# Spacer tiles between the moving operands of the four large products of an attention and two-layer feed-forward kernel

## The chip, the cores and the metric

One core of one Trainium2 chip runs the whole program. The metric is the device time in microseconds; lower is better. TensorE (PE) does the matrix products, VectorE (DVE), ScalarE (ACT) and GpSimd (POOL) the elementwise work, and SyncE (SP) issues the DMAs.

## The reference

```python
scores = scale * np.matmul(q, k.transpose(0, 1, 3, 2))       # 4 batches, 8 heads, 576 tokens, 64 wide
scores = np.where(block_i >= block_j, scores, -1000000000.0)  # blocks of 64 tokens
attn = np.exp(scores - np.max(scores, axis=-1, keepdims=True))
attn = attn / (np.sum(attn, axis=-1, keepdims=True) + 1e-09)
x = np.matmul(attn, v).transpose(0, 2, 1, 3).reshape(2304, 512)
...
g = x @ w_gate                                                # 512 x 1536
x = (g / (1 + np.exp(-g)) * (x @ w_val)) @ w_out              # 1536 x 512
...
h = x @ w_in                                                  # 512 x 2048
out = np.where(h > 0, h, np.exp(np.minimum(h, 0)) - 1) @ w_out2   # 2048 x 512
```

All tensors are float32.

## The kernel before

The 2304 tokens are worked on in three phases. Every large product is made three times as precise as one pass by splitting both operands into a high and a low part (float32r): `mm3` (lines 163 to 166) issues high weights times high operand (L164), high weights times low operand (L165) and low weights times high operand (L166). For TensorE one operand is stationary (the "weights", 128 columns, loaded by an LDWEIGHTS ahead of the matmul) and one is moving (streamed through, up to 512 columns). While a matmul streams its moving operand, the next matmul's weights are loaded.

- Phase 1, to about 482 us: attention, and the product **gv** (gate and value, `gv_pair`). It goes over 9 chunks of 256 tokens; the moving operand is `xh` or `xl` (a tile of 4 x 256 columns, three buffers of each, chunk c uses buffer c mod 3), the weights are `wh` and `wl`.
- Phase 2, to about 655 us: the product **y** (`p2_unit`): five chunks, four of 512 and one of 256 tokens. The moving operand is `ah` or `al` (three buffers each), the weights `woh` and `wol`. Meanwhile `p3_weights` prepares weights for phase 3.
- Phase 3, to the end: the products **h** and **o**, over 3 groups of 768 tokens and 8 pairs of 128 hidden columns. h (`p3_h`) is written as seven products of halves (a Strassen-like scheme): the moving operand is `yo0` to `yo6` (384 columns of a high or low part), the weights are streamed slots `ws`, six matmuls for each of the seven. o (`p3_o`, L891 to L893) has the second layer's weights `oh`/`ol` as the moving operand (512 columns) and the activations `gh`/`gl` (the last three of eight buffers are `ah`/`al` again) as the stationary one. o trails h by one step, and runs of the two alternate.

The order of all instructions on all engines is fixed by `Plan.order`, a planner with costs written in the kernel; it knows nothing of addresses. Addresses come from pools that are filled tile after tile from either end of the memory. A tile that takes the place of an older one waits for the older one's readers. In this kernel all weights of the four products start at 128 bytes modulo 512. `padr` (352 bytes), `padx` (192) and `padw` (320) are tiles that nobody reads: they shift what is allocated behind them.

Of the kernel before, what the change touches and what calls it, by code (L numbers as in the profile page):

```python
# [8 lines left out]
F32 = mybir.dt.float32  # L9
F32R = mybir.dt.float32r  # L10
# [11 lines left out]
KD, K1, K2 = DM // 128, F1 // 128, F2 // 128  # L22
BLK = 64
CH = 256
# [13 lines left out]
HT, NG, HP, PAIR3, NP, NW, NE = 384, 3, K2 // 2, 15.4, 8, 8, 3  # L38
# [72 lines left out]
def attention_moe_moe_kernel(ctx: ExitStack, tc: tile.TileContext,  # L111
# [9 lines left out]
    def sb(name, bufs, side="left"):  # L121
        return tc.alloc_tile_pool(name=name, bufs=bufs, side=side, reuse_waits="tile")

    def ps(name, bufs, side="left"):
        return tc.alloc_tile_pool(name=name, bufs=bufs, side=side, space=PSUM, reuse_waits="tile")

    const = sb("const", 1)
    ident = const.tile([128, 128], F32, name="ident")
    conv = sb("conv", 1)
# [82 lines left out]
    pl_t = {g: [attn.tile([128, e], F32, name=f"pl{g}{i}") for i in range(2)] for g, e in ((0, 256), (1, 512))}  # L212
    ph_t = [attn.tile([128, S], F32, name=f"ph{i}") for i in range(2)]
    x_p = sb("x", 1)
    x_p.tile([128, 48], F32, name="padx")
    ph1 = sb("ph1", 1)
    ph1.tile([128, 80], F32, name="padw")
    t0 = sb("t0", 1)
    lo_r, hi_r = slice(0, 64), slice(64, 128)
    xh_c, xl_c = {}, {}  # L220

    def x_alloc(c):
        if c not in xh_c:
            xh_c[c] = x_p.tile([128, KD, CH], F32R, tag="xh", name="xh", bufs=3)
            xl_c[c] = x_p.tile([128, KD, CH], F32R, tag="xl", name="xl", bufs=3)


    def conv_unit(i, prio, after=(), whole=False):
# [54 lines left out]
    def t0_attn(s, q):  # L283
# [50 lines left out]
        def x(p):  # L334
            x_alloc(0)
            cs = slice(128 * s, 128 * s + 128)
            xh, xl = (t[0][:, 2 * q:2 * q + 2, cs].rearrange("p j (u t) -> p u j t", u=2) for t in (xh_c, xl_c))
            src = st["pv"][:, :, 0:128].rearrange("p u (j t) -> p u j t", j=2)
            if p == 0:
                act.copy(xh, src)  # L340
            else:
                dve.tensor_tensor(xl, src, xh.bitcast(F32), ALU.subtract)
# [48 lines left out]
    def a_head(n, prio):  # L391
# [199 lines left out]
        def xh():  # L591
            x_alloc(ch)
            act.copy(xh_c[ch][:, k], xfs[i])
# [4 lines left out]
        if fp:  # L598
            def fh():
                x_alloc(ch)  # L600
                act.copy(xh_c[ch][xr, k], st["pv"][0:64, 0:QW])

            def fl():
                dve.tensor_tensor(xl_c[ch][xr, k], st["pv"][0:64, 0:QW], xh_c[ch][xr, k].bitcast(F32), ALU.subtract)  # L604

            add("ACT", 264, fh, prio, [pvk], [("x", ch, ("h", k))])
            add("DVE", 335, fl, prio, [pvk, ("x", ch, ("h", k))], [("x", ch, ("l", k))])
            return
# [46 lines left out]
    ar_b, ah_b, al_b, ys_b = [], [], [], []  # L655
# [74 lines left out]
    def w2_alloc(p, f):  # L730
        OH[f] = p.tile([128, DM], F32R, name=f"oh{f}")
        OL[f] = p.tile([128, DM], F32R, name=f"ol{f}")
        cv_units[unit["o", f]] = (w2o[f], OH[f], OL[f])
# [190 lines left out]

    def p2_bufs(p, r, h):
        ar_b.extend(p.tile([128, 512], F32, name=f"ar{k}") for k in r)
        ah_b.extend(p.tile([128, 512], F32R, name=f"ah{k}") for k in h)
        al_b.extend(p.tile([128, 512], F32R, name=f"al{k}") for k in h)

    def to_w1():  # L930
        attn.release()
        at_ps.release()
        hand["st2"] = sb("st2", 1, "right")
        p2_bufs(hand["st2"], (0, 1, 2), (0, 1, 2))
        hand["w1"] = sb("w1", 1, "right")
        hand["y_ps"] = ps("y_ps", 1, "right")
        for g in range(K1 - 1):
            wo_alloc(hand["w1"], g)

    def wo_alloc(p, g):  # L940
        WOH[g] = p.tile([128, DM], F32R, name=f"woh{g}")
        WOL[g] = p.tile([128, DM], F32R, name=f"wol{g}")
        cv_units[2 * K1 + g] = (wo[g], WOH[g], WOL[g])

    def to_p2():
        hand["wgvB"].release()
        ph1.release()
        x_p.release()
        wgvA.release()
        gv_ps.release()  # L950
        hand["st3"] = sb("st3", 1)
        p = hand["st3"]
        p2_bufs(p, (3, 4), ())
        wo_alloc(p, K1 - 1)
        ys_b.extend(p.tile([128, 512], F32, name=f"ys{k}") for k in range(4))
        p = hand["wp"] = sb("wp", 1)
        for f in range(2 * NE):
            w2_alloc(p, f)
        for r in range(4):
            yqt[r] = p.tile([128, 2, HT], F32, name=f"yq{r}")  # L960
        for o in range(6):
            yot[o] = p.tile([128, 2, 2, HT], F32R, name=f"yo{o}")
        hand["h_ps"] = ps("h_ps", 1)
        for k in range(2):
            hb[k] = hand["h_ps"].tile([128, 512], F32, name=f"h{k}")

    def to_p3():
        hand["w1"].release()
        hand["y_ps"].release()
        p = hand["wq"] = sb("wq", 1, "right")  # L970
        yot[6] = p.tile([128, 2, 2, HT], F32R, name="yo6")
        for f in range(2 * NE, K2):
            w2_alloc(p, f)
        for k in range(NP):
            gp[k] = [t[k - NP + 3][:, 0:HT] for t in (ah_b, al_b)] if k >= NP - 3 else [p.tile([128, HT], F32R, name=f"g{h}{k}") for h in "hl"]
        hand["o_ps"] = ps("o_ps", 1, "right")
        for j in range(6):
            ob[j] = hb[j + 2] = hand["o_ps"].tile([128, DM], F32, name=f"o{j}")
# [5 lines left out]
    for c, f in order:  # L984
        u = UNIT0 if c < 2 else UNIT
# [38 lines left out]
    for u, (c, f) in enumerate(order):  # L1024
# [4 lines left out]
        plan.group = None  # L1029
    add("NONE", 0, to_w1, PT0, writes=[("w1", 0, 0)], behind="attn")  # L1030
    add("NONE", 0, to_p2, PT0, writes=[("p2", 0, 0)], behind="gv")
    for g in range(K1):
        conv_unit(2 * K1 + g, due2[0, g] - CLEAD2, after=[("w1" if g < K1 - 1 else "p2", 0, 0)])
# [5 lines left out]
    for i, T in chunks:  # L1039
        for f in range(K1):  # L1040
            p2_unit(i, T, f, p2_prep(i, T, f), due2[i, f])
        p2_drain(i, T)
    add("NONE", 0, to_p3, PT0, writes=[("p3", 0, 0)], behind="p2")
    for p in range(NE, HP):
        for f in (2 * p + 1, 2 * p):
# [66 lines left out]
```

## Time and profile before

| | us |
|---|---|
| median of 3 runs | 1047.3 |
| lowest, highest | 1046.73, 1049.97 |
| span of the profiled execution, first to last instruction | 1045.0 |
| PE busy, share of the span | 98% |
| weight loads busy | 89% |
| DVE busy | 79% |

The span is the profiled execution's own time on the core; 2.3 us lie between it and the median. Recorded matmuls overlap (they are pipelined, and the ends are modelled), so that a matmul's duration is longer than the time from its start to the next one's start. The mean of a group is in nanoseconds.

### The profile page before, as it was taken

The numbers are of one execution on the slowest core, as the hardware profiler recorded it, in microseconds if no ns is written. First come the engines' busy times: TensorE is split into PE (matmuls) and PEld (weight loads), VectorE is DVE, ScalarE is ACT, GpSimd is POOL, SyncE is SP. The second block draws the span as 40 slices with busy tenths as digits, with TensorE's granted clock in tenths as the row PEclk, the third lists the DMA queues.
The fourth block names the chain that finished last, engine by engine and source line by source line (L and its number), as shares of the span: only waits on it lengthen the run. The fifth ranks groups of instructions, "written<-read, shape, count | busy, mean of one in ns | idle before, by whom it ended". The sixth has DMA issues, their size and how long they took to land.

```text
span 1045.0 us, 19569 instructions
## 1 busy us (share of the span) xinstructions
PE 1023.0 (98%) x6520; PEld 935.1 (89%) x6520; DVE 825.7 (79%) x1967; ACT 606.3 (58%) x1531; POOL 286.5 (27%) x288
## 2 busy tenths in 40 slices
PE   9999899999999999999999999999999999999998
PEld 8678899999999999999977888898888998898897
DVE  6889999988888888877666775889998666876665
ACT  3898787776776677654354555555563443543343
POOL 1267543443444344303233222223210000000000
PEclk9999999999999999999999999999999999999999
DMA  7577557422542254004779988777646433454331
GB/s 177 163 217 207 154 160 202 122 80 87 139 123 81 85 140 122 25 28 134 227 258 321 316 292 282 252 237 235 218 149 211 126 121 121 122 172 121 112 111 61
DMA packets 119366, 170.00 MB, mean 163 GB/s; under 512 B 15840, under 2 KB 75744, under 8 KB 119264
## 3 DMA queue, kind: packets, MB, share of 16 engines
q1 hardware_dynamic: 119264, 168.74, 53.3%
q8 instruction: 52, 0.85, 0.3%
q14 instruction: 50, 0.41, 0.1%
HBM read 130.42 MB, written 38.27 MB: 161 GB/s over the span
## 4 chain that ended last, share of the span: by engine, by line
PE 79%; DVE 11%; DMA 4%; ACT 2%; issue 2%; SPq 1%; POOL 0%; ACTq 0%; DVEq 0%; POOLq 0%
PE gv L164 8%; PE gv L166 7%; PE gv L165 7%; PE o L893 6%; PE o L892 6%; PE o L891 6%; PE h L165 5%; PE h L166 5%; PE h L164 5%; PE y L165 3%; PE y L164 3%; PE y L166 3%; PE tr L534 2%; PE tr L533 2%; PE pv L551 2%
## 5 line engine op out<-in xcount | busy, mean ns | idle before, releaser
L164 PE MATMUL gv<-xh,wh 128*128 128x256 f32 x864 | 255.8, 296 | 0.2
L165 PE MATMUL gv<-xl,wh 128*128 128x256 f32 x864 | 241.7, 280 | 0.1
L166 PE MATMUL gv<-xh,wl 128*128 128x256 f32 x864 | 241.4, 279 | 0.0
L164 PEld LDWEIGHTS gv<-xh,wh 128*128 128x128 f32 x864 | 163.6, 189 | 4.8 <-issue 3.4
L165 PEld LDWEIGHTS gv<-xl,wh 128*128 128x128 f32 x864 | 163.8, 190 | 0.5 <-DVE xl L604 0.3
L166 PEld LDWEIGHTS gv<-xh,wl 128*128 128x128 f32 x864 | 163.3, 189 | 0.2 <-POOL wl L161 0.2
L853 DVE TENSOR_TENSOR ys<-h,ys 128x384 f32<-128x384 f32 x162 | 88.1, 554 | 69.1 <-PE h L166 66.3
L844 ACT ACTIVATE ar<-ys 128x384 f32<-128x384 f32 x96 | 50.4, 525 | 113.0 <-DVE ys L853 94.9
L165 PE MATMUL h<-yo,ws 128*128 128x384 f32 x326 | 110.1, 338 | 0.6 <-DVE yo L757 0.6
L164 PE MATMUL h<-yo,ws 128*128 128x384 f32 x326 | 109.3, 335 | 0.6 <-ACT ys L864 0.6
L166 PE MATMUL h<-yo,ws 128*128 128x384 f32 x326 | 109.6, 336 | 0.0
L409 POOL TENSOR_TENSOR ks<-rk,ks 64x576 fp32r<-64x576 f32 (+1 forms) x56 | 70.6, 1261 | 90.6 <-ACT ks L406 49.5
L165 PE MATMUL y<-al,woh 128*128 128x512 f32 (+1 forms) x240 | 89.0, 371 | 1.3 <-DVE al L669 1.1
L164 PE MATMUL y<-ah,woh 128*128 128x512 f32 (+1 forms) x240 | 88.5, 369 | 0.2 <-ACT ys L708 0.2
L166 PE MATMUL y<-ah,wol 128*128 128x512 f32 (+1 forms) x240 | 88.4, 368 | 0.0
L803 POOL TENSOR_TENSOR wm<-c,wm 128x256 fp32r<-128x256 f32 x56 | 50.6, 910 | 130.9 <-ACT wm L800 122.9
L538 ACT CAST th<-tr 128x256 fp32r<-128x256 f32 x176 | 61.3, 375 | 24.2 <-PE tr L534 22.8
L542 DVE TENSOR_TENSOR tl<-tr,th 128x256 fp32r<-128x256 f32 x176 | 69.0, 415 | 7.2 <-ACT th L538 6.5
L422 POOL TENSOR_TENSOR vs<-rv,vs 128x320 fp32r<-128x320 f32 (+1 forms) x56 | 47.2, 844 | 96.6 <-ACT vs L418 81.6
L892 PE MATMUL o<-ol,gh 128*128 128x512 f32 x180 | 71.2, 395 | 1.4 <-POOL ol L161 1.4
L893 PE MATMUL o<-oh,gl 128*128 128x512 f32 x180 | 71.5, 397 | 0.8 <-DVE gl L850 0.8
L891 PE MATMUL o<-oh,gh 128*128 128x512 f32 x180 | 70.2, 390 | 0.2 <-ACT oh L157 0.2
(149 smaller groups left out, 2673.5 us busy)
## 6 DMA issues: line engine op xcount, KB each, us to landing
ws<-w_scr SPq DMA_DIRECT2D x168, 256.0 KB, 2.7
w_scr<-wm SPq DMA_DIRECT2D x56, 256.0 KB, 3.9
a_scr<-as SPq DMA_DIRECT2D x54, 256.0 KB, 2.3
ar<-a_scr SPq DMA_DIRECT2D x108, 128.0 KB, 3.7
rk<-in_kt_dram SPq DMA_DIRECT2D x32, 288.0 KB, 4.4
raw<-in_w2i_dram SPq DMA_DIRECT2D x16, 512.0 KB, 4.7
raw<-in_w2o_dram SPq DMA_DIRECT2D x16, 512.0 KB, 4.3
rq<-in_qt_dram SPq DMA_DIRECT2D x60, 128.0 KB, 3.9
```

The costliest lines, as they stand in the source:

```text
L164: pe.matmul(dst, wh, xh, start=start, stop=False)
L165: pe.matmul(dst, wh, xl, start=False, stop=False)
L166: pe.matmul(dst, wl, xh, start=False, stop=stop)
L409: pool.tensor_tensor(st["ks"][64:128, 0:ext], raws[i][0][64:128, j, 0:ext], st["ks"][64:128, 0:ext].bitcast(F32), ALU.subtract)
L538: act.copy(st["th", c], st["tr", c][:, 0:QW])
L542: dve.tensor_tensor(st["tl", c], st["tr", c][:, 0:QW], st["th", c].bitcast(F32), ALU.subtract)
L803: add("POOL", 1000, lambda: pool.tensor_tensor(wm[n][:, 1], part(*x), wm[n][:, 0].bitcast(F32), ALU.subtract), prio, [ck(*x), hk] + whole, ...
L844: add("ACT", 500, lambda: act.activation(t(), src(), ACTF.Tanh, scale=0.5), PMP, [sk], [tk], first)
L853: add("DVE", 560, lambda: dve.tensor_tensor(hc(d), hb[b][:, 0:HT], hc(x), ALU.add), PMP, [hbk(b), hck(x)], [hck(d)])
L891: pe.matmul(d, h, OH[f], start=(p == 0 and u < 2), stop=False)
L892: pe.matmul(d, h, OL[f], start=False, stop=False)
L893: pe.matmul(d, l, OH[f], start=False, stop=(p == HP - 1 and u > 1))
```

## The change

`padx` and `padw` go. In their place stand small tiles between the buffers of the moving operands: 64 bytes between most, 32 or 128 between some. The x buffers, which were two rotating tags, become six named tiles in the order high 0, 1, 2, low 0, 1, 2. The spacers of each region come to 512 bytes, so that the weights behind them stay at 128 modulo 512 (ah and al, which o takes as weights, do not). Distances from the start of the moving operand to the start of the weights that are loaded while it streams, modulo 512 bytes, as the built programs have them:

| product | matmuls | before | after |
|---|---|---|---|
| gv, moving xh (L164, L166) | 1728 | 192 | 0, 64, 128 by buffer |
| gv, moving xl (L165) | 864 | 192 | 256, 320, 384 by buffer |
| y, moving ah | 480 | 0 | 64, 128, 192 by buffer |
| y, moving al | 240 | 0 | 320, 384, 448 by buffer |
| h, moving yo0 to yo6 | 1008 | 0 | 64, 128, 192, 256, 320, 384, 0 |
| o, moving oh, ol, by hidden column block | 864 | 0 | 0 for blocks 0 to 5 and 15, 32 to 448 for blocks 6 to 14; shifted again where ah or al are the weights |

Attention's own matmuls keep their distances, except where their weights are loaded behind a gv matmul. The instructions of every engine and their order are the same in both programs. What the new addresses change beside the distances are waits on tiles that stood there before. On POOL, where phase 2's weights are split (the first rows of phase 2; wol is the low part, the names in brackets are the queues and engines that an instruction waits for), before:

```order
L161 TENSOR_TENSOR wol0_8179<-c_2257,woh0_8178 128x512 [waits DVE_49,PE_49,Activation_49]
L161 TENSOR_TENSOR wol1_8181<-c_2273,woh1_8180 128x512 [waits DVE_49,PE_49,Activation_49]
L161 TENSOR_TENSOR wol2_8183<-c_2650,woh2_8182 128x512 [waits DMAHW6_49,Activation_49]
L161 TENSOR_TENSOR wol3_8185<-c_2672,woh3_8184 128x512 [waits DMAHW7_49,Activation_49]
L161 TENSOR_TENSOR wol4_8187<-c_8241,woh4_8186 128x512 [waits Activation_49]
```

and in the change:

```order
L168 TENSOR_TENSOR wol0_8179<-c_2262,woh0_8178 128x512 [waits DVE_49,PE_49,Activation_49]
L168 TENSOR_TENSOR wol1_8181<-c_2278,woh1_8180 128x512 [waits DVE_49,PE_49,Activation_49]
L168 TENSOR_TENSOR wol2_8183<-c_2655,woh2_8182 128x512 [waits DVE_49,DMAHW6_49,PE_49,Activation_49]
L168 TENSOR_TENSOR wol3_8185<-c_2675,woh3_8184 128x512 [waits DMAHW7_49,Activation_49]
L168 TENSOR_TENSOR wol4_8187<-c_8241,woh4_8186 128x512 [waits Activation_49]
```

Only wol2's row differs: it waits for DVE and PE as well. On SP the first load of ar1 gives its wait for PE and POOL to the first load of ar2, two rows later.

```diff
@@ -124,6 +124,13 @@
+    pads = [0]
+
+    def pad(p, n):
+        if n:
+            pads[0] += 1
+            p.tile([128, n // 4], F32, name=f"pad{pads[0]}")
+
@@ -212,17 +219,20 @@
     x_p = sb("x", 1)
-    x_p.tile([128, 48], F32, name="padx")
+    x_t = []
+    for h in "hl":
+        for u in range(3):
+            x_t.append(x_p.tile([128, KD, CH], F32R, name=f"x{h}{u}"))
+            pad(x_p, 128 if (h, u) == ("h", 2) else 64)
     ph1 = sb("ph1", 1)
-    ph1.tile([128, 80], F32, name="padw")
+    pad(ph1, 64)
...
     def x_alloc(c):
         if c not in xh_c:
-            xh_c[c] = x_p.tile([128, KD, CH], F32R, tag="xh", name="xh", bufs=3)
-            xl_c[c] = x_p.tile([128, KD, CH], F32R, tag="xl", name="xl", bufs=3)
+            xh_c[c], xl_c[c] = x_t[c % 3], x_t[3 + c % 3]
@@ -924,8 +934,11 @@
     def p2_bufs(p, r, h):
         ar_b.extend(p.tile([128, 512], F32, name=f"ar{k}") for k in r)
-        ah_b.extend(p.tile([128, 512], F32R, name=f"ah{k}") for k in h)
-        al_b.extend(p.tile([128, 512], F32R, name=f"al{k}") for k in h)
+        for b, x in ((ah_b, "h"), (al_b, "l")) if h else ():
+            for k in h:
+                pad(p, 128 if (x, k) == ("l", 0) else 64)
+                b.append(p.tile([128, 512], F32R, name=f"a{x}{k}"))
+        pad(p, 64 if h else 0)
@@ -959,7 +972,9 @@
         for o in range(6):
+            pad(p, 64)
             yot[o] = p.tile([128, 2, 2, HT], F32R, name=f"yo{o}")
+        pad(p, 128)
@@ -970,7 +985,9 @@
         for f in range(2 * NE, K2):
+            pad(p, 32 if f in (2 * NE, 2 * NE + 1, 2 * NE + 6, 2 * NE + 7) else 64)
             w2_alloc(p, f)
+        pad(p, 32 - 32 + 0)
```

## Rows read from the trace of the kernel before

**Rows 1.** The page: busy us, share of the span; granted clock by slice.

```profile
PE 1023.0 (98%) x6520; PEld 935.1 (89%) x6520; DVE 825.7 (79%) x1967; ACT 606.3 (58%) x1531; POOL 286.5 (27%) x288
...
PEclk9999999999999999999999999999999999999999
```

**Rows 2.** The page: the chain that ended last, by engine and by line.

```profile
PE 79%; DVE 11%; DMA 4%; ACT 2%; issue 2%; SPq 1%; POOL 0%; ACTq 0%; DVEq 0%; POOLq 0%
PE gv L164 8%; PE gv L166 7%; PE gv L165 7%; PE o L893 6%; PE o L892 6%; PE o L891 6%; PE h L165 5%; PE h L166 5%; PE h L164 5%; PE y L165 3%; PE y L164 3%; PE y L166 3%; PE tr L534 2%; PE tr L533 2%; PE pv L551 2%
```

**Rows 3.** Busy time of each engine by stretch (columns as the first row).

```profile
core 0: us, PE busy (x) PEld busy (x) DVE busy (x) ACT busy (x) POOL busy (x), PEclk, DMA share, GB/s
20.00:480.00 460.00, 448.91 (x3592) 426.89 (x3592) 401.27 (x1206) 336.01 (x973) 199.84 (x196) 1.00 0.45 126
480.00:515.00 35.00, 35.00 (x280) 33.61 (x280) 27.48 (x51) 13.62 (x27) 10.36 (x8) 1.00 0.55 169
515.00:655.00 140.00, 138.51 (x656) 114.92 (x655) 92.22 (x139) 68.80 (x136) 39.84 (x41) 1.00 0.86 292
655.00:1045.00 390.00, 382.38 (x1911) 342.24 (x1909) 294.25 (x543) 182.74 (x386) 34.34 (x31) 1.00 0.51 158
```

**Rows 4.** Line L165 in 495 to 505 and 279.3 to 282.2 us: ns min/median/max.

```profile
L165 PE MATMUL gv<-xl,wh x30: 276/276/276, 495.0 to 504.9; 128*128 128x256 f32 x30
L165 PE MATMUL gv<-xl,wh x9: 281/281/281, 279.3 to 282.1; 128*128 128x256 f32 x9
```

**Rows 5.** Lines L164, L165, L166 of gv from 20 to 482 us.

```profile
L164 PE MATMUL gv<-xh,wh x785: 276/281/561, 24.0 to 481.8; 128*128 128x256 f32 x197
L165 PE MATMUL gv<-xl,wh x784: 276/281/415, 24.2 to 480.8; 128*128 128x256 f32 x196
L166 PE MATMUL gv<-xh,wl x784: 276/280/415, 24.6 to 480.9; 128*128 128x256 f32 x196
```

**Rows 6.** Groups by shape on PE: busy us, mean ns, idle before.

```profile
L164 PE MATMUL gv<-xh,wh 128*128 128x256 f32 x864 | 255.8, 296 | 0.2
L165 PE MATMUL gv<-xl,wh 128*128 128x256 f32 x864 | 241.7, 280 | 0.1
L166 PE MATMUL gv<-xh,wl 128*128 128x256 f32 x864 | 241.4, 279 | 0.0
L165 PE MATMUL h<-yo,ws 128*128 128x384 f32 x326 | 110.1, 338 | 0.6 <-DVE yo L757 0.6
L166 PE MATMUL h<-yo,ws 128*128 128x384 f32 x326 | 109.6, 336 | 0.0
L164 PE MATMUL h<-yo,ws 128*128 128x384 f32 x326 | 109.3, 335 | 0.6 <-ACT ys L864 0.6
L893 PE MATMUL o<-oh,gl 128*128 128x512 f32 x180 | 71.5, 397 | 0.8 <-DVE gl L850 0.8
L892 PE MATMUL o<-ol,gh 128*128 128x512 f32 x180 | 71.2, 395 | 1.4 <-POOL ol L161 1.4
L891 PE MATMUL o<-oh,ah 128*128 128x512 f32 x108 | 42.0, 389 | 0.0
```

**Rows 7.** Line L165, 643.9 to 650 us: y at 256 columns.

```profile
L165 PE MATMUL y<-al,woh x18: 283/283/283, 643.8 to 649.9; 128*128 128x256 f32 x18
L165 PEld LDWEIGHTS y<-al,woh x17: 192/192/192, 644.0 to 649.8; 128*128 128x128 f32 x17
...
L165 PEld LDWEIGHTS gv<-xl,wh x30: 187/188/188, 494.9 to 504.7; 128*128 128x128 f32 x30
```

**Rows 8.** Line L165, 600 to 605 us: y at 512 columns.

```profile
L165 PE MATMUL y<-al,woh x7: 389/389/389, 600.3 to 604.4; 128*128 128x512 f32 x7
L165 PEld LDWEIGHTS y<-al,woh x8: 187/187/188, 600.1 to 604.8; 128*128 128x128 f32 x8
```

**Rows 9.** Matmuls with no load behind them: timeline, and ns min/median/max.

```profile
524.99 0.39 PE L164 MATMUL y<-ah,woh 128*128 128x512 f32 x1
525.21 0.19 PEld L165 LDWEIGHTS y<-al,woh 128*128 128x128 f32 x1 [0.26 <-DVE al L669]
...
L164 PE MATMUL y<-ah,woh x3: 388/389/393, 524.3 to 525.8; 128*128 128x512 f32 x3
...
L893 PE MATMUL o<-oh,al x8: 388/389/389, 1035.9 to 1040.6; 128*128 128x512 f32 x8
...
L893 PE MATMUL o<-oh,al x1: 388/388/388, 1040.6 to 1040.6; 128*128 128x512 f32 x1
```

**Rows 10.** h and o over the third phase: ns min/median/max.

```profile
L164 PE MATMUL h<-yo,ws x326: 331/334/446, 659.5 to 1030.8; 128*128 128x384 f32 x163
...
L893 PE MATMUL o<-oh,al x108: 387/397/398, 686.3 to 1040.6; 128*128 128x512 f32 x108
```

**Rows 11.** The first splits of wol on POOL, and wol's first matmuls.

```profile
474.13 5.25 POOL L161 TENSOR_TENSOR wol<-c,woh 128x512 fp32r<-128x512 f32 x4 [27.43 <-ACT woh L157]
483.72 1.29 POOL L161 TENSOR_TENSOR wol<-c,woh 128x512 fp32r<-128x512 f32 x1 [4.35 <-ACT woh L157]
...
L166 PE MATMUL y<-ah,wol x31: 387/389/398, 481.5 to 529.7; 128*128 128x512 f32 x31
```

## The prediction

> **What bounds the kernel now.** The page comes first: TensorE is busy 98% of a span of 1045.0 us, its weight loads 89%, VectorE 79%, and the granted clock is nine tenths or more in all 40 slices, the upper of its two levels [rows 1]. The chain of work that ended last is 79% PE, and its largest lines are the three matmuls of each product, gv, o, h and y [rows 2]. The table of stretches says the same stage by stage: PE is busy 448.9 of 460 us, 35.0 of 35, 138.5 of 140 and 382.4 of 390, while VectorE, the next engine, stays at 401 of 460 at most [rows 3]. So a change in the time of one matmul goes into the end almost one for one, and nothing else has to be counted unless VectorE has less than its 59 us left in the first stretch.
>
> How long is one matmul? The recorded durations overlap, so the reader has to see which part repeats. In the stretch from 495 to 505 us each line of gv shows 30 matmuls of 276 ns, the first starting at 495.0 and the last at 504.9 [rows 4]: 29 steps of three matmuls, so 9.9 us / 87 = 114 ns from start to start. The other 162 ns is the pipeline, covered by the next one. At 279 us nine show 281 ns, from 279.3 to 282.1, 2.8 / 24 = 117 ns [rows 4]. A matmul that is recorded 5 ns longer thus costs about 4 to 5 ns more of PE, and differences of durations are differences of cost. Over the whole of gv the minimum is 276 and the median 280 or 281 [rows 5]; the means of the two lines not hit by attention work ahead of them are 280 and 279 [rows 6]. gv has two habits, therefore, at one and the same distance (192).
>
> The y product has a part with the same 256 columns at distance 0: 18 matmuls of 283 ns from 643.8 to 649.9 us, 6.1 / 51 = 120 ns, with weight loads of 192 ns where gv's good habit has 188 [rows 7]. That is the best sign that distance may matter: 276 or 281 at 192, 283 at 0.
>
> With wider operands the sign is gone. y at 512 columns, also distance 0, shows 389 ns and weight loads of 187 or 188 [rows 8]. At 524.99 us such a matmul runs with no weights loaded meanwhile, since the next load waits for VectorE and starts at 525.21, and its record is the minimum of its three, 388; the very last matmul of the kernel, behind which no weights are loaded at all, is 388 too [rows 9]. Without any load there is nothing to collide with, and 1 ns is all that it saves. h and o, both at distance 0, spread: h has 331 to 334 at the least and means of 335, 338 and 336; o has 387 or 388 at the least and means from 389 to 397 [rows 6, 10].
>
> **The change, part by part.** No instruction is added, removed or moved. Every engine's list is the same, only addresses differ. Room is not at stake: each region's spacers come to 512 bytes per partition, so weights stay where they were modulo 512 (but for ah and al, which o also takes as weights). Three waits shift with the addresses: the split of wol2 on GpSimd also waits for PE and VectorE, which are then past the last attention head, and the load of ar2 takes over the wait that ar1 had. GpSimd makes its first four wol in one run from 474.13 us and is then idle 4.35 us; y's matmuls with wol begin at 481.5 [rows 11]. I cost them at nothing; should wol2 slip past its use, 1.3 us, the length of one split, is what is lost.
>
> All else is the price of a distance, and the trace shows three distances (192 in gv, 0 in the other three products, and attention's mixed ones, which are never in a steady run). I bound each product by its nearest rows.
>
> gv, 3 x 864 = 2592 matmuls. Now 279.5. Lower bound 276, upper bound 283, the same 256 columns at distance 0. That is 3.5 ns x 2592 = 9.1 us either way. The new distances are 0, 64 and 128 for xh and 256, 320 and 384 for xl, and 192 is not among them. For xh at 0 (chunks 0, 3, 6; two of three lines: 2592 x 1/3 x 2/3 = 576) I take the row at 0: 3.5 x 576 = +2.0 us. For the other 2016 no row is nearer to one end, so the middle, 279.5, and no change.
>
> y, 576 at 512 columns: 389 with a load, 388 without, so at best -0.6 us; taken as 0. The 144 at 256 columns go from 283 to the middle, -0.5 us (0 to -1.0).
>
> h, 1008 matmuls (326 per line, and 10 more per line that the first pass writes to o's banks). Mean 336.3; all at 331 would give -5.3 us, all at 338 +1.7. o, 3 x 288 = 864. Mean 393.3; all at 388 gives -4.6 us, all at 397 +3.2. Their short and long cases stand at one distance, 0, so distance is not what tells them apart. The short ones of o come in an unbroken run of o (the last eight of L893 are 388 or 389 [rows 9]); the long ones where h and o alternate, which the change keeps. I take both as unchanged.
>
> Sum: +2.0 - 0.5 = +1.5 us on a span of 1045.0, with 2.3 us around it to the median of 1047.3: **1048.8 us**. If every bound falls low: -9.1 - 1.0 - 0.6 - 5.3 - 4.6 = -20.6; if every one falls high: +9.1 + 1.7 + 3.2 = +14.0.
>
> The Trainium skill ("TensorE: Matmul & The Clock Gate", Step-by-step: what each phase is for) says that PE reads the moving operand and the weights through two independent ports, so that loading the next weights takes nothing from the running matmul. By that rule the sum is 0 and the time 1047.3. The 388 against 389 agrees; the 283 against 276 at equal width does not, or needs another cause.
>
> **The rivals.** First, *gv loses its place* (slower). 192 is a good distance and the ones near 0 behave as 0 does: xh in all chunks (1728 matmuls) goes to 283, +6.0 us, less 0.5 in y: 1052.8; with xl too, 1056. For it: 283 and the loads of 192 ns at distance 0 [rows 7]. Against: gv itself sits at 281 for long stretches, so 283 need not be the distance. It decides from 1.2 ns per gv matmul on (3.1 us / 2592).
>
> Second, *0 was the bad distance* (faster). The aligned start in h, o and y is what makes their matmuls long: h at 331, o at 388, y's narrow part at 276 give -5.3 - 4.6 - 1.0 = -10.9; with gv at +2.0, 1038.4. For it: all three products have means above their minima, and all stand at 0. Against: the 388 without a load.
>
> Third, *it does nothing*: all distances cost alike, the two habits of gv come from what ran before, and the time stays at 1047.3.
>
> **How the numbers follow.** The forecast (small terms that nearly cancel) has 0.30, the first rival 0.28, the second 0.28, the third 0.14. A measurement of this kernel can tell about 0.3%, 3.1 us, from no change. Same: 0.14 and most of the forecast, 0.37 with what the rivals leave below their points; slower 0.33; faster 0.30. To leave out no more than 2 in 10 the range must reach both outer rivals and beyond their middle prices: 1038 to 1057. The likeliest case alone has 1045 to 1052.
>
> **What would show it.** Right: gv of chunks 0, 3 and 6 with xh records near 283, the other chunks mixed between 276 and 283; y at 512 columns still 388 or 389; h and o with the means they have. First rival: gv's median at 282 or more in every chunk. Second: o's L892 and L893 near 388 and h's mean near 331. Third: every group within 1 ns of its row here. The prediction is wrong if a distance that no row shows (256 to 448) is far better or worse than both ends that I used, or if a distance that changes from one matmul to the next has a cost of its own; no steady row of this trace has that.

## The result, and the profile after

The changed kernel takes a median of 1051.5 us (20 executions, 1048.92 to 1061.75), the kernel before 1047.16 beside it. The ratio is 1.0061 (95% interval 1.0042 to 1.0080): slower by 0.6%. One of the 20 executions of the kernel before, 2015.79 us, lies far outside the rest. The profiled execution of it has a span of 1053.7 us, the one shown of before 1045.0.

The page of the changed kernel, busy time and granted clock, as in [rows 1]:

```profile
PE 1031.4 (98%) x6520; PEld 940.0 (89%) x6520; DVE 826.6 (78%) x1967; ACT 605.8 (57%) x1531; POOL 285.8 (27%) x288
...
PEclk8999999999999999999999999999999999999999
```

PE works 8.4 us more on the same 6520 matmuls; VectorE, ScalarE and GpSimd move by less than 1 us. One slice, the first, lost its full clock, so the next view is the table of stretches of the changed kernel: first the start, then the four stretches of [rows 3] (columns as there).

```profile
15.00:20.00 5.00, 4.18 (x20) 3.37 (x21) 3.74 (x12) 2.09 (x6) 0.00 (x0) 0.74 0.63 140
20.00:26.00 6.00, 6.00 (x26) 5.12 (x25) 3.25 (x13) 3.68 (x12) 2.77 (x2) 0.50 0.37 130
26.00:40.00 14.00, 13.86 (x64) 9.46 (x64) 9.72 (x31) 8.94 (x27) 2.56 (x2) 0.82 0.34 102
...
20.00:480.00 460.00, 449.92 (x3539) 427.55 (x3539) 395.74 (x1193) 331.07 (x963) 195.34 (x194) 0.99 0.44 125
480.00:515.00 35.00, 35.00 (x293) 34.84 (x292) 27.66 (x48) 14.31 (x29) 11.94 (x10) 1.00 0.47 144
515.00:655.00 140.00, 138.50 (x613) 111.59 (x612) 94.17 (x138) 67.75 (x132) 39.65 (x40) 1.00 0.86 283
655.00:1045.00 390.00, 385.82 (x1958) 346.57 (x1957) 293.44 (x546) 184.29 (x392) 36.73 (x34) 1.00 0.52 160
```

From 20 to 26 us the granted clock is 0.50, the lower of the two levels (1.2 GHz). The kernel before had 1.00 there, with PE as busy up to then (13.1 of the first 15 us here, 13.2 there). The mean clocks of the changed kernel's 20 executions reach from 0.984 to 1.000; by a straight line through them 0.001 of mean clock is 0.8 us, so that the profiled execution, at 0.994, holds some 3 us more of it than that of before, at 0.998. Matmul for matmul (their order is the same in both), the 150th starts 2.0 us later than before, and so does the 400th. So of the 8.7 us between the two spans about 2 come from the start and are not the change's; the medians differ by 4.3, the ratio says 6.4.

To place the rest, the last starts of gv, h and y in the line of low weights, kernel before and then the changed one (ns min/median/max, first and last start):

```profile
L166 PE MATMUL gv<-xh,wl x864: 276/279/415, 24.6 to 509.0; 128*128 128x256 f32 x173
L166 PE MATMUL h<-yo,ws x326: 334/334/346, 659.8 to 1031.1; 128*128 128x384 f32 x163
L166 PE MATMUL y<-ah,wol x240: 283/389/402, 481.5 to 659.4; 128*128 128x512 f32 x96, 128*128 128x256 f32 x24
```

```profile
L173 PE MATMUL gv<-xh,wl x864: 274/281/415, 23.1 to 514.7; 128*128 128x256 f32 x173
L173 PE MATMUL h<-yo,ws x326: 331/336/346, 668.4 to 1039.7; 128*128 128x384 f32 x163
L173 PE MATMUL y<-ah,wol x240: 274/393/404, 486.1 to 667.9; 128*128 128x512 f32 x96, 128*128 128x256 f32 x24
```

The last gv starts 5.7 us later (514.7 against 509.0), of which 2.0 are the start's. From there to the last y it is 153.2 us against 150.4, 2.8 more; from the last y to the last h 371.8 against 371.7. So in these two executions the loss lies in gv and y, nothing in h and o. The part of y is less sure than it looks: the same stretch took 148.9 to 152.0 us in other executions with y's distances of before, and 153.2 in one (experiment 3). The groups by shape of the changed kernel, which answer to [rows 6] (busy us, mean ns, idle before):

```profile
L171 PE MATMUL gv<-xh,wh 128*128 128x256 f32 x864 | 257.5, 298 | 0.2
L172 PE MATMUL gv<-xl,wh 128*128 128x256 f32 x864 | 243.5, 282 | 0.1
L173 PE MATMUL gv<-xh,wl 128*128 128x256 f32 x864 | 243.5, 282 | 0.0
...
L172 PE MATMUL y<-al,woh 128*128 128x512 f32 x192 | 76.2, 397 | 1.5 <-DVE al L679 1.4
L173 PE MATMUL y<-ah,wol 128*128 128x512 f32 x192 | 75.6, 394 | 0.0
L171 PE MATMUL y<-ah,woh 128*128 128x512 f32 x192 | 75.6, 394 | 0.0
...
L903 PE MATMUL o<-oh,gl 128*128 128x512 f32 x180 | 71.0, 394 | 0.8 <-DVE gl L860 0.8
...
L172 PE MATMUL y<-al,woh 128*128 128x256 f32 x48 | 13.5, 282 | 0.1
L171 PE MATMUL y<-ah,woh 128*128 128x256 f32 x48 | 13.5, 281 | 0.3 <-ACT ah L676 0.3
L173 PE MATMUL y<-ah,wol 128*128 128x256 f32 x48 | 13.4, 278 | 0.0
```

Two lines of y in the kernel before:

```profile
L166 PE MATMUL y<-ah,wol 128*128 128x512 f32 x192 | 74.8, 390 | 0.0
...
L166 PE MATMUL y<-ah,wol 128*128 128x256 f32 x48 | 13.6, 283 | 0.0
```

gv: 282 where it was 280 and 279. y at 512 columns: 394 to 397 where it was 390 to 393. y at 256 columns: 278 to 282 where it was 283. So the same distances shorten a product of 256 columns that stood at 0, lengthen one of 256 columns that stood at 192, and lengthen one of 512 columns that stood at 0.

gv, chunk by chunk, the line of xl in the changed kernel: a stretch at distance 0 (256 for xl), one at 64 (320), and the last, unbroken one at 128 (384):

```profile
L172 PE MATMUL gv<-xl,wh x44: 278/283/283, 375.8 to 397.3; 128*128 128x256 f32 x44
...
L172 PE MATMUL gv<-xl,wh x16: 278/279/280, 456.5 to 464.8; 128*128 128x256 f32 x16
...
L172 PE MATMUL gv<-xl,wh x70: 279/281/285, 490.0 to 514.6; 128*128 128x256 f32 x70
```

283 at 0, 279 at 64, 281 at 128; the 276 of the last stretch before [rows 4] is gone. It is not gone everywhere: at 64 some short stretches between attention's matmuls keep it, the longest 16 steps of 113.3 ns.

```profile
L172 PE MATMUL gv<-xl,wh x6: 276/276/276, 73.9 to 75.6; 128*128 128x256 f32 x6
```

For prices it is better to take the time from one start to the next, which doesn't rest on modelled ends. The trace's starts, put beside the addresses in the built programs, give the mean over matmuls that follow five others of the same product, width and distance; steps over 30 ns above the median are left out as waits. The table is modulo 256 and holds runs of the experiments too. In gv distances 256 apart (xh at 0 with xl at 256, 64 with 320) gave the same within 1 ns, but there the two alternate. In h whole groups of six matmuls stand at one distance, and in the changed kernel they say the same within about 1 ns: 176.5 ns at 0 and at 256, 173.1 at 64 and 172.8 at 320, 174.6 at 128 and 175.7 at 384. ns from start to start:

| distance | gv, 256 columns | y, 256 columns | y, 512 columns |
|---|---|---|---|
| 0 | 119.5 | 120.0 | 227.0 |
| 32 | 117.0 | 117.2 | 233.3 |
| 64 | 117.1 | 117.8 | 229.1 |
| 128 | 118.8 | 118.1 | 232.4 |
| 160 | 117.9 | 118.1 | 234.3 |
| 192 | 113.3 or 117.8 (mean 115.1 to 116.1) | 113.4 or 117.8 | 233.4 |
| 224 | 118.3 | 117.8 | 233.2 |

At 256 columns 0 is the worst distance of all and 192 the best where it holds its short pace; at 512 columns 0 is the best of all. Now the sum for the change, from the mean steps over all matmuls of a group (steps more than 40 ns too long left out as waits): gv from 116.0 to 118.3, 2.3 x 2592 = +6.0 us; y at 512 columns 4.6 x 576 = +2.6; y at 256 columns -3.4 x 144 = -0.5; h -0.2; o +0.4; together +8.3 of PE time. The experiments ask what of it is distance, and what of it reaches the end.

### The profile page after: what moved, and what is told of

Same layout as the page of the kernel before. It is cut to its first block, busy times and chain, and to the rows that moved or that the text cites. A ratio compares the mean times of both kernels' runs of the same rounds, so it can differ in the third digit from the quotient of the medians.

```text
span 1053.7 us, 19570 instructions
## 1 busy us (share of the span) xinstructions
PE 1031.4 (98%) x6520; PEld 940.0 (89%) x6520; DVE 826.6 (78%) x1967; ACT 605.8 (57%) x1531; POOL 285.8 (27%) x288
## 4 chain that ended last, share of the span: by engine, by line
PE 69%; DVE 14%; DMA 9%; ACT 3%; issue 2%; SPq 2%; POOL 0%; DVEq 0%; ACTq 0%; POOLq 0%
PE gv L171 8%; PE gv L173 7%; PE gv L172 7%; PE o L903 6%; PE o L902 6%; PE o L901 6%; PE h L172 5%; PE h L171 5%; PE h L173 5%; DMA w_scr<-wm 2%; DMA ar<-a_scr 2%; DVE c L159 2%; DVE c L161 2%; PE tr L544 2%; PE tr L543 2%
```

## The experiments

**1. Everything moved, no distance changed.** A spacer of 64 bytes ahead of all tiles on one side, and 64 bytes less in `padr` on the other.

```diff
+    const.tile([128, 16], F32, name="padc")
...
-    padr.tile([128, 88], F32, name="padr")
+    padr.tile([128, 72], F32, name="padr")
```

> The kernel before with every tile 64 bytes further on (a 64-byte tile behind the identity, padr 64 bytes smaller): all distances as before, all positions 64 bytes higher. Theory A (the distance from the moving operand to the weights, modulo 256, sets the time of a matmul): nothing changes; L165 of gv has a mean of 280 ns with minimum 276, y at 512 columns 389 in its steady stretch, y at 256 columns 283, span about 1045. Theory B (the position of the moving operand alone, modulo 256, sets it): x moves to where y's operand stood and y to where it stands with distance 64 after the change, so gv goes to about 283, y at 512 columns to about 391, y at 256 columns to about 281, and the span to about 1054. Theory C (the changed waits of the new addresses, not the matmuls, cost the time): no forecast for the durations, PE's idle time before y grows.

Measured: 1042.85 us in one execution, beside a median of 1045.23 (13 executions, 1040.91 to 1053.0) of the kernel before. Groups by shape:

```profile
L166 PE MATMUL gv<-xl,wh 128*128 128x256 f32 x864 | 241.7, 280 | 0.1
L167 PE MATMUL gv<-xh,wl 128*128 128x256 f32 x864 | 241.4, 279 | 0.0
...
L165 PE MATMUL y<-ah,woh 128*128 128x512 f32 x192 | 74.7, 389 | 0.0
```

The means of [rows 6], and y's 390, within 1 ns. Where the operands stand by themselves does nothing.

**2. The same, but x stays where it was.** gv's distance becomes 128, x's own address is that of before.

```diff
-    x_p.tile([128, 48], F32, name="padx")
+    x_p.tile([128, 32], F32, name="padx")
...
-    ph1.tile([128, 80], F32, name="padw")
+    ph1.tile([128, 96], F32, name="padw")
```

> As the run before, but the x buffers stay where they were, so that gv's distance is 128 instead of 192 while x's own position is unchanged; all else is 64 bytes further on with its old distances. Theory A: gv's two undisturbed lines go from 280 and 279 to 282 (what the change has at 128), y stays at 389 and 283, span about 1050. Theory B: gv stays at 280 and 279, y goes to about 391 and 281. The two shifted runs together separate distance from position in both products.

Measured: 1049.17 us in one execution, 6.3 above experiment 1, from which it differs in x alone.

Groups by shape:

```profile
L167 PE MATMUL gv<-xh,wl 128*128 128x256 f32 x864 | 244.2, 283 | 0.0
L166 PE MATMUL gv<-xl,wh 128*128 128x256 f32 x864 | 244.0, 282 | 0.1
```

gv lengthens by 2 to 4 ns though its moving operand did not move; y keeps 390 to 392. It is the distance.

**3. The x spacers alone.** The change's first two parts; ah, al, yo, oh and ol as before.

```diff
-    x_p.tile([128, 48], F32, name="padx")
+    x_t = []
+    for h in "hl":
+        for u in range(3):
+            x_t.append(x_p.tile([128, KD, CH], F32R, name=f"x{h}{u}"))
+            pad(x_p, 128 if (h, u) == ("h", 2) else 64)
...
-    ph1.tile([128, 80], F32, name="padw")
+    pad(ph1, 64)
...
```

> The changed kernel with the spacers of x alone; y, h and o at distance 0 as before. Theory A: gv at 282 ns as in the change (+2.3 ns on 2592 matmuls, about +6 us), y back at 389 to 390 and 283; the span about 1051, the median ratio to the kernel before about 1.005. If only waits matter (theory C), the ratio stays at 1.000 to 1.002, since the waits that moved belong to y's spacers.

Measured: 1050.8 us, ratio 1.0055 (1.0023 to 1.0087). Groups by shape: gv 281, and y at 512 columns back at 390 where it doesn't wait.

```profile
L173 PE MATMUL gv<-xh,wl 128*128 128x256 f32 x864 | 243.1, 281 | 0.0
...
L173 PE MATMUL y<-ah,wol 128*128 128x512 f32 x192 | 74.9, 390 | 0.0
```

gv alone gives nearly the whole of 1.0061. y waited longer in this profile than before (3.4 us against 1.3), though nothing of y was changed.

**4. Odd multiples of 32.** All spacers of the change laid out anew so that the distances are 32, 160 and 224 modulo 256 (h and o mixed).

```diff
+    for n in (32, 128, 64, 64, 128, 64):
+        pad(x_p, n)
+        x_t.append(x_p.tile([128, KD, CH], F32R, name=f"x{len(x_t)}"))
...
```

> Other distances, all odd multiples of 32 modulo 256: gv 32, 160 and 224 by chunk (chunks 0, 3, 6; 1, 4, 7; 2, 5, 8), y 32, 160 and 224 by buffer, h 32 to 352 in steps of 64. Theory A as a smooth function of distance with the change's values (gv steady: 0 worst, 192 best; y at 512 columns: 0 best, 192 worst): gv at 160 and 224 between 276 and 281, at 32 about 282; y at 512 columns 390 at 32, about 396 at 160 and 393 at 224; y at 256 columns about 279 on average. If what counts is a multiple of 64 (a line), odd multiples of 32 fall into the class of their lower neighbour: gv at 224 like 192, at 160 like 128, at 32 like 0.

Measured: 1050.09 us in one execution. Groups by shape: gv 281, y at 512 columns 396 or 397, worse than expected.

```profile
L172 PE MATMUL gv<-x,wh 128*128 128x256 f32 x864 | 242.6, 281 | 0.1
...
L172 PE MATMUL y<-al,woh 128*128 128x512 f32 x192 | 76.1, 396 | 0.4 <-DVE al L678 0.4
```

The table above has its values. 32 lies between 0 and 64 and does not behave so: at 512 columns it costs 233.3 where both neighbours cost less, so neither form that was expected for the curve fits.

**5. Which weights?** High weights at 192 from x, low weights at 0, by allocating all high tiles, a spacer of 192 bytes, and all low tiles.

```diff
+                WH[f, m] = p.tile([128, KD, 128], F32R, name=f"wh{f}_{m}")
+        p.tile([128, 48], F32, name=f"padl{fs[0]}")
...
+                WL[f, m] = p.tile([128, KD, 128], F32R, name=f"wl{f}_{m}")
```

> In gv all high weights stand at distance 192 from x as in the kernel before, and all low weights are moved by 192 bytes more, to distance 0 from x. A matmul has two sets of weights near it: its own, loaded ahead of it, and the next ones, loaded while it streams. Theory A1 (the load that runs meanwhile counts): the line that moves xl, during which the low weights are loaded, goes from 280 to 283 ns or more (the mean of y's 256 columns at distance 0), the two lines that move xh stay at 279 to 280; 864 matmuls at 3 to 5 ns, +2.6 to +4.3 us. Theory A2 (its own weights count): the line xh with low weights lengthens by 3 to 5 ns and the other two stay. If neither line lengthens alone, the distance acts on more than one matmul. y, h and o stand at shifted places here and are not read.

Measured: 1048.5 us in one execution. The last stretch of gv, its three lines:

```profile
L164 PE MATMUL gv<-xh,wh x77: 281/281/282, 481.8 to 508.7; 128*128 128x256 f32 x77
...
L165 PE MATMUL gv<-xl,wh x77: 282/282/283, 481.9 to 508.8; 128*128 128x256 f32 x77
...
L166 PE MATMUL gv<-xh,wl x77: 280/281/282, 482.0 to 508.9; 128*128 128x256 f32 x77
```

No line lengthens alone; all three stand at 281 or so, 117.8 ns from start to start, as gv at 192 does in its long habit (experiment 6). One matmul in three at another distance seems to keep the short habit away (one execution): 7% of gv's steps are under 115.7 ns here, 43% in the kernel before, and 30 to 44% in all eight traces with gv at 192. Whether the own or the next weights count stays open.

**6. The ah and al spacers alone, twice.**

```diff
+        for b, x in ((ah_b, "h"), (al_b, "l")) if h else ():
+            for k in h:
+                pad(p, 128 if (x, k) == ("l", 0) else 64)
+                b.append(p.tile([128, 512], F32R, name=f"a{x}{k}"))
...
```

> The kernel before with the spacers between the ah and al buffers alone. Distance theory: y at 512 columns leaves its 389 to 390 ns for 394 or so as in the changed kernel (about 4.6 ns more from start to start, 576 matmuls, +2.7 us), y at 256 columns goes from 283 to 278 to 282 (-0.5 us), gv and h keep 280 and 336: +2 us, a ratio of 1.002. Rival (y's extra time came with gv's new addresses or from the waits of the second stretch): y stays at 389 to 390 and the time is that of the kernel before.

Measured: 1049.94 us, ratio 1.0051 (1.0018 to 1.0084), more than expected. The matmuls did what the distance theory says (y at 512 columns 394 and 395, at 256 columns 278 and 279), but that is 2 us, not 5. Two things stood out. The eight executions had a mean clock of 0.993, the 27 of before beside them 0.996. And gv's last stretch, at the unchanged distance 192, ran in the long habit, where before [rows 4] it ran in the short one (the line of xl, ns min/median/max, here and in the kernel before):

```profile
L172 PE MATMUL gv<-xl,wh x79: 281/281/282, 480.9 to 508.5; 128*128 128x256 f32 x79
```

```profile
L165 PE MATMUL gv<-xl,wh x80: 276/276/280, 482.1 to 508.9; 128*128 128x256 f32 x80
```

240 matmuls at 4.4 ns, 1.1 us. Experiment 1's trace had the long habit there too. So the kernel was run again, in more executions:

> The kernel with the ah and al spacers alone once more, in more rounds, because its first ratio (1.0051) and that of y at distance 192 alone (1.0001) don't fit each other: both lengthen y's wide matmuls by 2.7 to 3.8 us in their profiles, and the executions of the first were granted a lower mean clock (0.993) than those of the kernel before beside them (0.996). If y's extra time is mostly taken out of y's waits for al and the rest was the clock: a ratio of 1.000 to 1.002. If y's extra time reaches the end: 1.003 or more. y's wide matmuls at 394 to 395 ns and its narrow ones at 278 to 279 in either case.

Measured: 1047.38 us, ratio 1.0006 (0.9986 to 1.0026). The same kernel again has y at 394, and the same line shows gv's last stretch in the short habit:

```profile
L172 PE MATMUL gv<-xl,wh x80: 276/276/282, 480.8 to 508.5; 128*128 128x256 f32 x80
```

So most of the first ratio was not the change of ah and al: by straight lines of time against mean clock, as for the changed kernel above, the two runs lie 1.1 and 0.7 us above the kernel before, each at the same mean clock (0.997). The second interval still leaves room for the expected 2 us.

**7. The yo, oh and ol spacers alone.**

```diff
+            pad(p, 64)
             yot[o] = p.tile([128, 2, 2, HT], F32R, name=f"yo{o}")
+        pad(p, 128)
...
+            pad(p, 32 if f in (2 * NE, 2 * NE + 1, 2 * NE + 6, 2 * NE + 7) else 64)
             w2_alloc(p, f)
```

> The kernel before with the spacers between yo0 to yo6 and between oh and ol alone. Theory: h at 337 and o at 394 ns, the same sums as before within 1 us, since each mixes better and worse distances; time within 0.1% of the kernel before. Rival (h and o share in the loss, hidden in the changed kernel by a gain elsewhere): 1 to 3 us more.

Measured: 1045.79 us, ratio 1.0014 (0.9997 to 1.0031). From start to start h keeps its mean within 0.1 ns and o too (in all 0.0 and -0.1 us). That is what the distance theory expected.

**8. A distance for each width.** gv at 192, y at 512 columns and o at 0 as before; yo0 to yo6 at 64; y's last chunk read from column 48 of ah and al, which is 192.

```diff
+        o = 0 if T > CH else 48
-            act.activation(ah_b[v % 3][:, 0:T], ar_b[u % 5][:, 0:T], ACTF.Copy, scale=0.5)
+            act.activation(ah_b[v % 3][:, o:o + T], ar_b[u % 5][:, 0:T], ACTF.Copy, scale=0.5)
...
+        p.tile([128, 16], F32, name="padh")
         for o in range(6):
             yot[o] = p.tile([128, 2, 2, HT], F32R, name=f"yo{o}")
+        p.tile([128, 112], F32, name="padi")
...
```

> A distance for each width, from what the runs so far show: gv stays at 192, y at 512 columns and o stay at 0, y's last chunk (256 columns) is read from column 48 of ah and al, which is distance 192, and yo0 to yo6 (h, 384 columns) go to distance 64. If the distance sets the time by width: y at 256 columns from 283 to 276 ns or so (144 matmuls at 6.5 ns, -0.9 us), h from a mean of 336.3 to 335 (1008 at 1.5 ns, -1.5 us), in all -2.5 us, a ratio of 0.998. Rival (the changes of h are noise of its own habits): y's 256 columns shorten, h stays at 336, -0.9 us at most.

Measured: 1041.46 us, ratio 0.9958 (0.9935 to 0.9982): faster than the kernel before, and by about 1% than the changed one (0.9958 / 1.0061). Groups by shape:

```profile
L166 PE MATMUL h<-yo,ws 128*128 128x384 f32 x326 | 109.4, 336 | 0.0
...
L895 PE MATMUL o<-oh,gl 128*128 128x512 f32 x180 | 70.8, 394 | 0.8 <-DVE gl L852 0.8
...
L166 PE MATMUL y<-ah,wol 128*128 128x256 f32 x48 | 13.4, 279 | 0.0
```

From start to start h lost 1.5 ns (-1.5 us), y at 256 columns 3.9 (-0.6 us) and o, at an unchanged distance, 1.7 (-1.5 us; 1.1 ns where the next matmul is an o as well): 3.6 of some 4.4 us. The recorded means of h do not show it (337, 336 and 336, where [rows 6] has 335, 338 and 336). The last h comes 370.0 us after the last y, not 371.7.

**9. gv at 0 throughout.**

```diff
-    x_p.tile([128, 48], F32, name="padx")
...
-    ph1.tile([128, 80], F32, name="padw")
+    ph1.tile([128, 128], F32, name="padw")
```

> One distance alone in gv, 0 in place of 192; y, h and o as before. Distance theory: the matmuls of gv go from 279 or 280 to 283 ns or so, the mean of y's 256 columns at distance 0; from start to start 12.6 us per thousand over the streaming time in place of 9.4 on average, as chunks 0, 3 and 6 of the changed kernel had: 3.2 to 3.6 ns x 2592 = +8 to +9 us if all of it reaches the end, a ratio of 1.008; half of that if the first stretch's idle time (11 us of 460) takes up a part. Rival (what lengthened gv in the changed kernel was that its distance changes from chunk to chunk): with one constant distance gv keeps 279 to 280 and the time that of the kernel before.

Measured: 1054.13 us, ratio 1.0062 (1.0036 to 1.0088). The last stretch of gv:

```profile
L165 PE MATMUL gv<-xl,wh x80: 280/283/283, 486.8 to 515.2; 128*128 128x256 f32 x80
```

28.4 us for 237 steps, 119.8 ns, where the 80 of before took 26.8 us (482.1 to 508.9), 113.1. Over all of gv 119.3 against 116.0, 3.3 x 2592 = +8.5 us of PE time, and the ratio says +6.5 (3.8 to 9.2). In the trace itself the stretch from the 150th matmul to the last gv takes 482.8 us, against 478.3 in the mean of the eight traces with gv at 192 (477.0 to 479.9): +4.5. A constant distance costs too, so it is not the change from chunk to chunk.

**10. y at 192 throughout.**

```diff
+            p.tile([128, 48], F32, name="pada")
         ah_b.extend(p.tile([128, 512], F32R, name=f"ah{k}") for k in h)
         al_b.extend(p.tile([128, 512], F32R, name=f"al{k}") for k in h)
...
+            p.tile([128, 80], F32, name="padb")
```

> One distance alone in y, 192 in place of 0; gv and h as before, three of o's eight weight buffers shifted. Distance theory with an order that turns round between the widths: y at 512 columns from 389 or 390 to 395 or 396 ns (576 matmuls, about 6.3 ns each, +3.6 us), y at 256 columns from 283 to 276 to 279 (144 matmuls, -0.6 to -1.0 us): +2.6 to +3 us, a ratio of 1.0025 to 1.003. Rival (a distance that changes from chunk to chunk is what costs): y at 512 columns stays at 389 to 390.

Measured: 1046.95 us, ratio 1.0001 (0.9975 to 1.0028). The wide matmuls did as the theory says, and the median time did not, though the interval reaches up to the expected ratio. One of their groups by shape, and then the third stretch:

```profile
L166 PE MATMUL y<-ah,wol 128*128 128x512 f32 x192 | 75.9, 395 | 0.0
```

```profile
515.00:655.00 140.00, 140.00 (x657) 115.31 (x657) 91.46 (x138) 68.67 (x136) 39.70 (x41) 1.00 0.87 291
```

PE has no idle time left there, where before it had 1.5 us [rows 3]. The waits that the kernel before had from 480 to 655 us (us in total, times, longest):

```profile
PE y L165 <- DVE al L669: 1.1, 2, 0.8
PE y L164 <- ACT ys L708: 0.2, 1, 0.2
```

A slower PE would come later to al, and find it ready. Counted from start to start, steps of y at 512 columns that are more than 40 ns too long held 3.2 us before and 0.1 us here, against 3.8 us more in the others, and from the last gv to the last y both executions take about the same (150.4 us before, 150.6 here). That the slower matmuls are what took the waits away is not shown: with y's distances of before, too, the waits differ from 0.2 to 3.4 us between executions.

**11. h at 64 alone**, experiment 8 without its y part.

```diff
+        p.tile([128, 16], F32, name="padh")
         for o in range(6):
             yot[o] = p.tile([128, 2, 2, HT], F32R, name=f"yo{o}")
+        p.tile([128, 112], F32, name="padi")
...
+        p.tile([128, 16], F32, name="padj")
         yot[6] = p.tile([128, 2, 2, HT], F32R, name="yo6")
...
+        p.tile([128, 112], F32, name="padk")
```

> The kernel by width without its y part: the kernel before with yo0 to yo6 at distance 64 alone. If h's distance is what shortened o in the kernel by width too (its o went from 389 to 397 down to 390 to 394 ns at an unchanged distance 0): h at 336 with fewer long cases (-1.5 us), o at 390 to 394 (-1.5 us), a ratio of 0.997. Rival (o's gain came from elsewhere or differs from execution to execution): o has 389 to 397 as before and the ratio is 0.9985 at the least.

Measured: 1044.3 us, ratio 0.9976 (0.9954 to 0.9997). From start to start h lost 1.5 ns as in 8, and o 1.9 ns (1.1 where the next matmul is an o as well). In recorded durations o's cases with ah and al are at 390 to 392 (389 to 395 before), those with gh and gl at 395 to 397: half of what was expected of o's rows.

## Why the prediction came out as it did

The range (1038 to 1057) held 1051.5, the forecast (1048.8) did not: the first rival, gv loses its place (1052.8), is what happened, for nearly the reason given for it. That its number comes so near is in part luck: it priced two thirds of gv's matmuls at 3.5 ns where all of them lost 2.3 on average, had nothing for y at 512 columns, and let all of it reach the end.

**What bounds the kernel** was too strict. "A change in the time of one matmul goes into the end almost one for one": in gv at 0, +8.5 us of PE time gave +6.5 by the ratio and +4.5 in the trace; in y at 192, +3.5 us gave nothing that the executions can tell (1.0001), and in the profile PE no longer waited for al. The prediction looked for an exception in the first stretch alone. The 1.5 us of idle time in the row of 515 to 655 us [rows 3] was the sign, and was passed over.

**gv** was mis-sized: +2.0 us forecast, +6.0 of PE time measured. xh at 0 came as priced (283, [rows 7]). The step that failed is "for the other 2016 no row is nearer to one end, so the middle, 279.5, and no change". At 128 gv does not mix the two habits of [rows 5]; it loses the short one. At 64 it keeps it in short stretches alone. The mean of before, 279.5, was itself a mean of 276 and 281, and the right question was how long another distance can hold 276. No unbroken stretch at another distance held the short pace for more than 16 steps in any run (and at 0, 32, 128, 160 and 224 for not even nine), where 192 held it for up to 237. The second error in the same step is xl, taken as another distance than xh's: 256 apart costs alike, so xl at 256 cost what xh cost at 0. And "differences of durations are differences of cost" held for gv but not for h, whose steps shortened in experiment 8 while its records did not.

**y at 512 columns**, "taken as 0", failed as a price (4.6 ns, +2.6 us of PE time). How much of it reaches the end stays open: the ratios of experiments 6 (second run) and 10, 1.0006 and 1.0001, point to little, but their intervals reach 2.7 and 2.9 us. One profile cannot say it, since y's waits differ by execution: they were 0 in experiment 10 and 0.7 us in the second run of 6, but 0.6 and 3.4 in 1 and 3, which have y's distances of before, and 1.7 in the changed kernel's profile, whose y was 2.8 us longer. The reasoning was: "without any load there is nothing to collide with, and 1 ns is all that it saves". It compared a matmul with a load and one without at distance 0 alone, which at this width is the best distance there is. In the changed kernel a matmul with no load behind it for 1.5 us is recorded as long as its neighbours (timeline, start and length in us):

```profile
606.51 0.39 PE L173 MATMUL y<-ah,wol 128*128 128x512 f32 x1
...
606.74 0.40 PE L171 MATMUL y<-ah,woh 128*128 128x512 f32 x1
608.22 0.19 PEld L172 LDWEIGHTS y<-al,woh 128*128 128x128 f32 x1 [1.52 <-DVE al L679]
```

It stands at 64 and takes 0.40 us (396 ns), where [rows 9] has 388 at 0. So in this one record, whose end is modelled, the load that runs behind a matmul is not what makes it long, and a matmul without one was no test of distance.

**y at 256 columns** was right, -0.5 us for -0.5. **h and o unchanged** was right for this change (-0.2 and +0.4 us of PE time, ratio 1.0014 alone). The sentence under it, "distance is not what tells them apart", was not: h at 64 shortens by 1.5 ns, and o shortens with it (experiments 8 and 11). The second rival had that much truth; its 10.9 us was far too much.

**The three waits**, costed at nothing, were nothing: from 480 us to the end of y PE waited 1.4 us for al and 0.3 for ah, 1.1 us for al and 0.2 for ys before, and for no wol.

**The third rival**, all distances alike, is out by experiments 2 and 9. It was weighed with the Trainium skill ("TensorE: Matmul & The Clock Gate", Step-by-step: what each phase is for): two independent ports, so that loading the next weights takes nothing from the running matmul, by which the time was 1047.3. The runs show that placement is not free: 276 and 283 at one width, by the distance alone. That the ports collide is not shown either, given the matmul without a load.

Adding up the parts does not close: 1.0055 for x, 1.0006 for y, 1.0014 for h and o, 1.0075 in all, against 1.0061; the intervals cover the difference.

What stays open: the mechanism. That it is the distance and not the place and that it depends on the width is shown, and that it repeats after 256 bytes for h; in gv and y the distances 256 apart always stood side by side. What holds gv in one of its two habits, which weights count, and why the order turns round between 256 and 512 columns, is not shown.

## What to carry to other kernels

Where PE is the bound and matmuls run back to back, the offset between the moving operand and the weights is a parameter to measure per width, worth 3% of a wide matmul here (227.0 to 234.3 ns) and 6% of a narrow one (113.3 to 120.0); one spacer rule for all products gives up in one what it gains in another. Before pricing a matmul by its mean, look whether the mean is one of two habits, and ask what holds the better one. And where PE waits even 1% of a stage, a longer matmul need not lengthen the stage by as much: read the idle time of that stage, not of the kernel, and of more than one execution.

## What was not expected of the hardware

At 256 columns distance 0 is the slowest (119.5 to 120.0 ns) and 192 can be the fastest (113.3); at 512 columns 0 is the fastest (227.0) and 160 the slowest (234.3). At 192 a run of narrow matmuls holds one of two paces, 276 or 281 recorded, over hundreds of matmuls with nothing in the program to tell them apart: the same kernel held 281 through its last stretch in one execution and 276 in the other (experiment 6); of the eight traces with gv at 192, six held 276 there and two 281. And with h at another distance, o shortened by 1.7 and 1.9 ns at its old one (experiments 8 and 11).
